# Softmax attention of one query, forward and backward: row broadcast ahead of the K scores, row maxima spread by one transpose, V chunks reordered

## The chip, the cores and the metric

The kernel runs on one core of a Trainium2 chip. The metric is the device time in microseconds, median of several executions. One execution of each kernel was also taken with the hardware profiler; its span is 1.7 to 2.9 us shorter than the time of the same execution. The granted clock is the share of full speed that the profile shows TensorE was granted.

## The reference

```python
B, H, Sq, Skv, Dh = 1, 32, 1, 8192, 128          # bfloat16
def fwd(q, k, v):
    scores = einsum('bhqd,bhkd->bhqk', q, k) * Dh ** -0.5
    return einsum('bhqk,bhkd->bhqd', softmax(scores), v)
def reference(q, k, v, grad_out):
    out, vjp = jax.vjp(fwd, q, k, v)
    return (out, *vjp(grad_out))                 # out, dq, dk, dv
```

A head has one query, 8192 keys and 8192 values. Each head reads K and V (2 MiB each) once and writes dK and dV (2 MiB each) once: 8.39 MB per head, 268.4 MB in all.

## The kernel before

A head's K and V lie on 128 partitions with 64 slots of 128 elements each. VectorE transposes K, TensorE makes the scores, softmax follows, TensorE transposes V in four chunks and makes the products with it, and VectorE writes dV = p x grad_out and dK = ds x q, which are stored. The program works on head h while it finishes dK of head h-1. In the profile lines, XK_sb is the transposed K, s_ps the scores, mx and nbias the row maxima, e the exponentials, qd the broadcast rows of q and grad_out, p_rep and ds_rep are p and ds, and G_dv and G_dk are dV and dK on their way out. The parts that the change touches (cut at the dots):

```python
def k_scores(h):
    x = st[h]
    x["s"] = psS.tile([P, 512], F32, tag="s", name="s_ps")     # one PSUM bank
    ...                                                        # 64 matmuls into x["s"][:, 0:NT]

def rows_bc(h):                                                # q and grad_out on all partitions
    x = st[h]
    nc.tensor.matmul(x["m"][:, 256:512], lhsT=ident[0:H, h:h + 1].to_broadcast([H, P]),
                     rhs=rows[:].rearrange("h a d -> h (a d)"), start=True, stop=True, ...)
    x["qd"] = small.tile([P, 2, D], BF16, tag="qd", name="qd")
    nc.scalar.copy(x["qd"][:].rearrange("p a d -> p (a d)"), x["m"][:, 256:512])

for h in range(H + 1):
    p_ = h - 1
    if h < H:
        x = st[h] = {}
        for u in range(NCH):
            k_blocks(h, u)                       # VectorE transposes of K
        k_scores(h)
    ...                                          # ds, first parts of dK and dq of head h-1
    if 0 < h and h + 2 < H:
        load_k(h + 2)                            # 3 K buffers
    if h < H:
        nc.vector.reduce_max(mx[:], x["sn"], axis=AX.X)
        nc.vector.tensor_scalar(diag[:], ident_f[:], mx[:], scale, op0=ALU.mult, op1=ALU.mult)
        nc.tensor.matmul(x["m"][:, 128:256], lhsT=ones_f[:], rhs=diag[:], ...)
        rows_bc(h)
    if h > 0:
        outer(p_, "dk", 2)
    if h < H:
        nc.vector.tensor_reduce(nbias[:], x["m"][:, 128:256], axis=AX.X, op=ALU.max, negate=True)
        nc.scalar.activation(e[:], x["sn"], ACT.Exp, bias=nbias[:], scale=scale, accum_out=rs[:])
    ...
    v_transposes(h, 0); v_transposes(h, 1)       # each: 8 transposes on TensorE, one ScalarE copy
    contract(Vt[h], x["p"], x["m"][:, 2:3])      # O: 64 matmuls
    v_scores(h, 0)
    v_transposes(h, 2)
    ...                                          # one product with grad_out
    v_scores(h, 1)
    v_transposes(h, 3)
    v_scores(h, 2); v_scores(h, 3)
    for r in range(4): outer(h, "dv", r)         # the store follows the last part
```

Of the kernel before, what the change touches and what calls it, by code (L numbers as in the profile page):

```python
# [9 lines left out]
ALU = mybir.AluOpType  # L10
AX = mybir.AxisListType
BF16 = mybir.dt.bfloat16
F32 = mybir.dt.float32
# [10 lines left out]
def kernel(  # L24
# [11 lines left out]
    nc = tc.nc  # L36
    P = 128
    _, H, S, D = k.shape
# [7 lines left out]
    scale = float(D) ** -0.5  # L46
# [7 lines left out]
    small = ctx.enter_context(tc.tile_pool(name="small", bufs=2))  # L54
    psT = ctx.enter_context(tc.tile_pool(name="psT", bufs=2, space=PSUM))
    psS = ctx.enter_context(tc.tile_pool(name="psS", bufs=1, space=PSUM))
# [19 lines left out]
    def load_v(h):  # L76
        Vt[h] = vpool.tile([P, NT, D], BF16, tag="V", name="Vt")
        nc.sync.dma_start(Vt[h][:], rows_of(v, h, 0, 1))
# [9 lines left out]
    ident = consts.tile([P, P], BF16)  # L88
# [5 lines left out]
    ones_f = consts.tile([P, P], F32)  # L94
# [19 lines left out]
    ident_f = consts.tile([P, P], F32)  # L114
# [10 lines left out]
    def do_columns():  # L125
        for e2 in range(2):
            nc.scalar.copy(
                twice[:, e2], rows[:, 1, :].rearrange("h (j e) -> h e j", e=2)[:, e2:e2 + 1, :].to_broadcast([H, 2, W]))
        tp = psT.tile([P, CH, P], BF16, tag="T", name="tp_do")
        for e2 in range(2):  # L130
            nc.tensor.transpose(tp[:, e2, 0:H], twice[:, e2].rearrange("h t j -> h (t j)"), ident[0:H, 0:H])
        nc.tensor.transpose(tp[:, 2, 0:H], rows[:, 1, :], ident[0:H, 0:H])
        for e2 in range(2):
            for t in range(2):
                nc.scalar.copy(do_blk[t * W:(t + 1) * W, :, e2, t], tp[t * W:(t + 1) * W, e2, 0:H])
        nc.scalar.copy(do_f[:], tp[:, 2, 0:H])
# [4 lines left out]
    def k_blocks(h, u):  # L141


        if u == 0:
            XK[h] = ktpool.tile([P, CH, NB, NCH, QD], F32, tag="XK", name="XK_sb")
        nc.vector.transpose(XK[h][:, :, :, u, :],  # L146
                            slots(Kt[h], u, NCH).rearrange("p g d -> p (g d)").bitcast(F32).rearrange(
                                "p (g w j) -> p g w j", g=CH, w=NB))

    def k_scores(h):  # L150
        x = st[h]
        x["s"] = psS.tile([P, 512], F32, tag="s", name="s_ps")
        out = x["s"][:, 0:NT].rearrange("p (a g) -> p g a", a=NQ)
        cols = XK.pop(h).rearrange("p g w u i -> p (g w u i)").bitcast(BF16).rearrange(
            "p (g w ui e) -> p g w e ui", g=CH, w=NB, e=2)
        for g in range(CH):
            for c in range(2 * NB):
                nc.tensor.matmul(out[:, g, :], lhsT=cols[:, g, c // 2, c % 2], rhs=q_blk[:, h, c, :],  # L158
                                 start=(c == 0), stop=(c == 2 * NB - 1), skip_group_check=True)
# [18 lines left out]
    def v_transposes(h, c):  # L178

        T_ps = psT.tile([P, CH // 2, P], F32, tag="T", name="T_ps")  # L180
        words = Vt[h].rearrange("p n d -> p (n d)").bitcast(F32)
        for i in range(CH // 2):
            m = c * CH // 2 + i
            nc.tensor.transpose(T_ps[:, i, :], words[:, m * P:(m + 1) * P], ident_f[:])  # L184
        X = tpool.tile([P, CH // 2, P], F32, tag="XT", name="XT_sb")
        nc.scalar.copy(X[:], T_ps[:])  # L186
        XV[h, c] = X

    def v_scores(h, c):
        X = XV.pop((h, c)).rearrange("p m s -> p (m s)").bitcast(BF16).rearrange("p (m s e) -> p m e s", s=P, e=2)  # L190
        if c == 0:
            st[h]["dp"] = psD.tile([P, 512], F32, tag="dp", name="dp_ps")
        for i in range(CH // 2):
            n = c * CH + 2 * i
            for e2 in range(2):
                nc.tensor.matmul(st[h]["dp"][:, n:n + 2], lhsT=X[:, i, e2, :], rhs=do_blk[:, h, e2, :],  # L196
                                 start=(e2 == 0), stop=(e2 == 1), skip_group_check=True)

    def contract(Xt, rep, out_col, first=0, last=NT):
        for n in range(first, last):  # L200
            nc.tensor.matmul(out_col, lhsT=Xt[:, n, :], rhs=rep[:, n, 0:1],  # L201
                             start=(n == 0), stop=(n == NT - 1), skip_group_check=True)
# [19 lines left out]

    def rows_bc(h):
        x = st[h]
        nc.tensor.matmul(x["m"][:, 256:512], lhsT=ident[0:H, h:h + 1].to_broadcast([H, P]),  # L225
                         rhs=rows[:].rearrange("h a d -> h (a d)"), start=True, stop=True,
                         skip_group_check=True)
        x["qd"] = small.tile([P, 2, D], BF16, tag="qd", name="qd")
        nc.scalar.copy(x["qd"][:].rearrange("p a d -> p (a d)"), x["m"][:, 256:512])  # L229

    def ds_of(h):
        x = st[h]
# [7 lines left out]
    def dq_of(h, half):  # L240
        out = st[h]["dp"][:, 128:129]
        contract(Kt[h], st[h]["ds"], out, half * NT // 2, (half + 1) * NT // 2)
        if half == 1:
            nc.scalar.copy(dq_all[:, h:h + 1], out)  # L244
# [10 lines left out]
    for h in range(H + 1):  # L255
        p_ = h - 1
        if h < H:
            x = st[h] = {}
            for u in range(NCH):
                k_blocks(h, u)  # L260
            k_scores(h)
        if h == 0:
            do_columns()
        if h > 0:
            ds_of(p_)
            outer(p_, "dk", 0)
            dq_of(p_, 0)
        if h < H:
            s_mask(h)
            s_swap(h)  # L270
        if h > 0:
            dq_of(p_, 1)
            outer(p_, "dk", 1)
        if 0 < h and h + 2 < H:
            load_k(h + 2)
        if h < H:
            mx = small.tile([P, 1], F32, tag="mx")
            nc.vector.reduce_max(mx[:], x["sn"], axis=AX.X)
            diag = small.tile([P, P], F32, tag="diag")
            nc.vector.tensor_scalar(diag[:], ident_f[:], mx[:], scale, op0=ALU.mult, op1=ALU.mult)  # L280
            x["m"] = psM.tile([P, 512], F32, tag="m", name="m_ps")
            nc.tensor.matmul(x["m"][:, 128:256], lhsT=ones_f[:], rhs=diag[:], start=True, stop=True,  # L282
                             skip_group_check=True)
            rows_bc(h)
        if h > 0:
            outer(p_, "dk", 2)
        if h == 0:
            load_k(2)
        if h < H:
            nbias = small.tile([P, 1], F32, tag="nbias")  # L290
            nc.vector.tensor_reduce(nbias[:], x["m"][:, 128:256], axis=AX.X, op=ALU.max, negate=True)  # L291
            e = small.tile([P, NT], F32, tag="e")
            rs = small.tile([P, 1], F32, tag="rs")
            nc.scalar.activation(e[:], x["sn"], ACT.Exp, bias=nbias[:], scale=scale, accum_out=rs[:])  # L294
            nc.tensor.matmul(x["m"][:, 0:1], lhsT=ones_f[:], rhs=rs[:], start=True, stop=True,  # L295
                             skip_group_check=True)
        if h > 0:
            outer(p_, "dk", 3)
        if h == H:
            break  # L300
        rinv = small.tile([P, 1], F32, tag="rinv")
        nc.vector.reciprocal(rinv[:], x["m"][:, 0:1])  # L302
        x["p"] = small.tile([P, NT, R], BF16, tag="prep", name="p_rep")
        nc.scalar.activation(x["p"][:], e[:].unsqueeze(2).to_broadcast([P, NT, R]), ACT.Copy, scale=rinv[:])  # L304
        x["p_s"] = small.tile([P, NT], F32, tag="p_s", name="p_s")
        nc.vector.tensor_scalar(x["p_s"][:], e[:], rinv[:], scale, op0=ALU.mult, op1=ALU.mult)
        v_transposes(h, 0)
        v_transposes(h, 1)
        contract(Vt[h], x["p"], x["m"][:, 2:3])
        nc.scalar.copy(o_all[:, h:h + 1], x["m"][:, 2:3])  # L310
        v_scores(h, 0)
        v_transposes(h, 2)
        nc.tensor.matmul(x["m"][:, 1:2], lhsT=do_f[:, h:h + 1].to_broadcast([P, P]), rhs=o_all[:, h:h + 1],
                         start=True, stop=True, skip_group_check=True)
        v_scores(h, 1)
        v_transposes(h, 3)
        v_scores(h, 2)
        v_scores(h, 3)
        outer(h, "dv", 0)
        outer(h, "dv", 1)  # L320
        outer(h, "dv", 2)
        if 0 < h and h + 2 < H:
            load_v(h + 2)
        outer(h, "dv", 3)
        if h == 0:
            load_v(2)
        if h == H - 1:
            result(o_all, out_0)
# [33 lines left out]
```

## Time and profile before

| | before |
|---|---|
| time, median of 3 runs | 647.68 us (646.88 to 647.79) |
| span of the profiled run | 646.4 us |
| busy: VectorE, TensorE, ScalarE | 79%, 77%, 29% |
| data moved, share of 16 DMA engines | 268.47 MB, 97.9% |

"Share of 16 DMA engines" adds the durations of all packets and divides by 16 spans. From the list of who waited for whom (waiter, what ended the wait, us in total, times, longest us):

```profile
PE s_ps L158 <- DVE pdt L234: 50.4, 25, 3.7
DVE nbias L291 <- ACT qd L229: 20.6, 32, 2.0
```

The first is TensorE idle ahead of the K scores. (The wait is for the K transposes; pdt is the VectorE instruction right after them.) The second is VectorE waiting for qd, the copy of the row broadcast.

### The profile page before, as it was taken

How to read it: one execution, taken by the hardware profiler on the slowest of the kernel's cores; microseconds unless marked ns; L12 is line 12 of the kernel's file. 1: busy time of each engine (PE TensorE's matmuls, PEld its weight loads, DVE VectorE, ACT ScalarE, POOL GpSimd, SP SyncE). 2: the span in 40 equal slices, each digit the busy share in tenths (PEclk: the TensorE clock that was granted, in tenths of full speed). 3: DMA queues.
4: the chain of work that ended last, by engine and by line, in shares of the span. 5: the costliest groups of instructions: out<-in, count | busy, mean ns of one | idle time of the engine just before them, and what ended most of it. 6: DMA issues, size and time to landing. Idle time of an engine off the chain costs nothing.

```text
span 646.4 us, 20967 instructions
## 1 busy us (share of the span) xinstructions
PE 500.6 (77%) x9705; PEld 468.8 (73%) x9705; DVE 512.2 (79%) x653; ACT 184.7 (29%) x332; POOL 0.7 (0%) x6
## 2 busy tenths in 40 slices
PE   2888888788879867788768698767787788877880
PEld 1888787688878756778757687767686787866880
DVE  5888889899877779777798777898777977778851
ACT  2333233233233222232222322223322223222230
POOL 0000000000000000000000000000000000000000
PEclk9765556766655656755566755576755555655555
DMA  8999999999999999999999999999999999999985
GB/s 341 415 426 427 427 420 425 431 424 426 427 428 428 427 431 424 427 430 428 427 428 431 425 427 429 429 429 426 427 429 426 428 429 428 425 429 430 409 358 216
DMA packets 19719, 269.81 MB, mean 417 GB/s; under 512 B 2352, under 2 KB 2352, under 8 KB 2864
## 3 DMA queue, kind: packets, MB, share of 16 engines
q1 hardware_dynamic: 19584, 268.47, 97.9%
q8 instruction: 76, 1.25, 0.7%
q14 instruction: 11, 0.09, 0.0%
q10 hardware_dynamic: 48, 0.01, 0.0%
HBM read 134.23 MB, written 134.23 MB: 415 GB/s over the span
## 4 chain that ended last, share of the span: by engine, by line
DMA 58%; PE 23%; DVE 13%; ACT 2%; issue 1%; SPq 0%; DVEq 0%; ACTq 0%
DMA Kt<-in_k_dram 58%; DVE XK_sb L146 10%; PE T_ps L184 6%; PE s_ps L158 6%; PE dp_ps L201 5%; PE m_ps L201 2%; DVE G_dv L211 1%; PE dp_ps L196 1%; PE s_ps L174 1%; ACT XT_sb L186 1%; PE m_ps L282 1%; DVE G_dk L211 1%; PE m_ps L295 1%; ACT qd L229 0%; PE m_ps L225 0%
## 5 line engine op out<-in xcount | busy, mean ns | idle before, releaser
L184 PE MATMUL T_ps<-ident_f,Vt 128*128 128x128 f32 x1024 | 216.2, 391 | 0.0
L211 DVE TENSOR_TENSOR G_dv<-p_rep,qd 128x2048 bf16<-128x2048 bf16 x128 | 148.2, 1220 | 68.7 <-DMA out_dram<-G_dv 66.5
L184 PEld LDWEIGHTS T_ps<-ident_f,Vt 128*128 128x128 f32 x1024 | 191.8, 213 | 0.0
L186 ACT COPY XT_sb<-T_ps 128x1024 f32<-128x1024 f32 x128 | 129.6, 1013 | 142.1 <-PE T_ps L184 142.1
L211 DVE TENSOR_TENSOR G_dk<-ds_rep,qd 128x2048 bf16<-128x2048 bf16 x128 | 155.7, 1218 | 1.1
L146 DVE STREAM_TRANSPOSE XK_sb<-Kt 128x1024 f32<-128x1024 f32 x128 | 148.2, 1214 | 7.4 <-DMA Kt<-in_k_dram 6.9
L158 PE MATMUL s_ps<-q_blk,XK_sb 128*128 128x4 bf16 x2048 | 59.5, 168 | 58.2 <-DVE pdt L234 50.4
L158 PEld LDWEIGHTS <-XK_sb 128*128 128x128 bf16 x2048 | 56.9, 104 | 60.4 <-DVE pdt L234 52.4
L196 PEld LDWEIGHTS <-XT_sb 128*128 128x128 bf16 x2048 | 71.7, 104 | 28.9 <-ACT XT_sb L186 27.4
L196 PE MATMUL dp_ps<-do_blk,XT_sb 128*128 128x2 bf16 x2048 | 72.7, 165 | 24.7 <-ACT XT_sb L186 24.7
L201 PE MATMUL dp_ps<-ds_rep,Kt 128*128 128x1 bf16 x2048 | 64.4, 165 | 2.9 <-issue 2.5
L201 PEld LDWEIGHTS <-Kt 128*128 128x128 bf16 x2048 | 59.7, 104 | 8.4 <-issue 8.2
L244 ACT COPY dq_all<-dp_ps 128x1 f32<-128x1 f32 x32 | 5.1, 159 | 199.9 <-PE dp_ps L201 199.9
L201 PEld LDWEIGHTS <-Vt 128*128 128x128 bf16 x2048 | 60.2, 101 | 1.5
L201 PE MATMUL m_ps<-p_rep,Vt 128*128 128x1 bf16 x2048 | 58.7, 165 | 0.0
L295 PEld LDWEIGHTS m_ps<-rs,ones_f 128*128 128x128 f32 x64 | 16.0, 311 | 48.6 <-ACT e L294 48.6
L295 PE MATMUL m_ps<-rs,ones_f 128*128 128x1 f32 x64 | 18.7, 362 | 39.2 <-ACT e L294 39.2
L282 PE MATMUL m_ps<-diag,ones_f 128*128 128x128 f32 x64 | 25.4, 501 | 0.7 <-DVE diag L280 0.7
L291 DVE TENSOR_REDUCE nbias<-m_ps 128x1 f32<-128x128 f32 x32 | 9.3, 292 | 20.6 <-ACT qd L229 20.6
L304 ACT ACTIVATE p_rep<-e,rinv 128x256 bf16<-128x256 f32 x32 | 16.3, 508 | 30.0 <-DVE rinv L302 30.0
L236 DVE SCALAR_TENSOR_TENSOR ds_rep<-dp_ps,pdt,p_s 128x256 bf16<-128x256 f32 x32 | 15.5, 484 | 11.3 <-PE dp_ps L196 8.7
L229 ACT CAST qd<-m_ps 128x256 bf16<-128x256 f32 x32 | 11.9, 372 | 30.5 <-PE m_ps L225 30.5
(44 smaller groups left out, 155.0 us busy)
## 6 DMA issues: line engine op xcount, KB each, us to landing
Vt<-in_v_dram SPq DMA_DIRECT2D x32, 2048.0 KB, 28.2
Kt<-in_k_dram SPq DMA_DIRECT2D x31, 2048.0 KB, 30.7
out_dram<-G_dv SPq DMA_DIRECT2D x30, 2048.0 KB, 32.8
out_dram<-G_dk SPq DMA_DIRECT2D x30, 2048.0 KB, 32.9
out_dram<-G_dv SPq DMA_DIRECT2D x4, 1024.0 KB, 14.0
out_dram<-G_dk SPq DMA_DIRECT2D x4, 1024.0 KB, 12.0
Kt<-in_k_dram SPq DMA_DIRECT2D x4, 512.0 KB, 5.5
out_dram<-fin_sb SPq DMA_DIRECT2D x2, 8.0 KB, 11.9
```

What stands on the lines that cost most here:

```text
L146: nc.vector.transpose(XK[h][:, :, :, u, :], slots(Kt[h], u, NCH).rearrange("p g d -> p (g d)").bitcast(F32).rearrange("p (g w j) -> p g w ...
L158: nc.tensor.matmul(out[:, g, :], lhsT=cols[:, g, c // 2, c % 2], rhs=q_blk[:, h, c, :], start=(c == 0), stop=(c == 2 * NB - 1), skip_group ...
L184: nc.tensor.transpose(T_ps[:, i, :], words[:, m * P:(m + 1) * P], ident_f[:])
L186: nc.scalar.copy(X[:], T_ps[:])
L196: nc.tensor.matmul(st[h]["dp"][:, n:n + 2], lhsT=X[:, i, e2, :], rhs=do_blk[:, h, e2, :], start=(e2 == 0), stop=(e2 == 1), skip_group_chec ...
L201: nc.tensor.matmul(out_col, lhsT=Xt[:, n, :], rhs=rep[:, n, 0:1], start=(n == 0), stop=(n == NT - 1), skip_group_check=True)
L211: nc.vector.tensor_tensor(slots(G, r, 4).rearrange("p n (a b) -> p n a b", b=R), slots(rep, r, 4).unsqueeze(2).to_broadcast([P, Q, D // R, ...
L229: nc.scalar.copy(x["qd"][:].rearrange("p a d -> p (a d)"), x["m"][:, 256:512])
L236: nc.vector.scalar_tensor_tensor(out=x["ds"][:], in0=x["dp"][:, 0:NT].unsqueeze(2).to_broadcast([P, NT, R]), scalar=pdt[:], in1=x["p_s"][: ...
L282: nc.tensor.matmul(x["m"][:, 128:256], lhsT=ones_f[:], rhs=diag[:], start=True, stop=True, skip_group_check=True)
L295: nc.tensor.matmul(x["m"][:, 0:1], lhsT=ones_f[:], rhs=rs[:], start=True, stop=True, skip_group_check=True)
L304: nc.scalar.activation(x["p"][:], e[:].unsqueeze(2).to_broadcast([P, NT, R]), ACT.Copy, scale=rinv[:])
```

## The change

The intent is to shorten the chain from the row maxima to the exponential, and to close gaps in the V part.

```diff
     def k_scores(h):
         x = st[h]
-        x["s"] = psS.tile([P, 512], F32, tag="s", name="s_ps")
@@ rows_bc
-        nc.tensor.matmul(x["m"][:, 256:512], lhsT=ident[0:H, h:h + 1].to_broadcast([H, P]),
+        x["s"] = psS.tile([P, 512], F32, tag="s", name="s_ps")
+        nc.tensor.matmul(x["s"][:, 256:512], lhsT=ident[0:H, h:h + 1].to_broadcast([H, P]),
...
-        nc.scalar.copy(x["qd"][:].rearrange("p a d -> p (a d)"), x["m"][:, 256:512])
+        nc.scalar.copy(x["qd"][:].rearrange("p a d -> p (a d)"), x["s"][:, 256:512])
@@ the loop over heads
             x = st[h] = {}
+            rows_bc(h)
             for u in range(NCH):
...
-            diag = small.tile([P, P], F32, tag="diag")
-            nc.vector.tensor_scalar(diag[:], ident_f[:], mx[:], scale, op0=ALU.mult, op1=ALU.mult)
+            top = small.tile([P, 1], F32, tag="top")
+            nc.vector.tensor_scalar_mul(top[:], mx[:], scale)
...
-            nc.tensor.matmul(x["m"][:, 128:256], lhsT=ones_f[:], rhs=diag[:], start=True, stop=True,
-                             skip_group_check=True)
-            rows_bc(h)
+            nc.tensor.transpose(x["m"][:, 128:256], top[:].to_broadcast([P, P]), ident_f[:])
...
         v_transposes(h, 1)
+        v_transposes(h, 2)
         contract(Vt[h], x["p"], x["m"][:, 2:3])
         nc.scalar.copy(o_all[:, h:h + 1], x["m"][:, 2:3])
         v_scores(h, 0)
-        v_transposes(h, 2)
+        v_scores(h, 1)
+        v_transposes(h, 3)
         nc.tensor.matmul(x["m"][:, 1:2], ...)
-        v_scores(h, 1)
-        v_transposes(h, 3)
         v_scores(h, 2)
```

## The prediction

> **What bounds the kernel now.** I read the page first: its DMA rows and its table of DMA queues.
>
> ```profile
> DMA  8999999999999999999999999999999999999985
> q1 hardware_dynamic: 19584, 268.47, 97.9%
> HBM read 134.23 MB, written 134.23 MB: 415 GB/s over the span
> ```
>
> The reader is to see that the 16 DMA engines are busy in every fortieth of the run but the first and the last two, and that the packets of the one data queue take 97.9% of 16 engines' time: 0.979 x 646.4 = 632.8 us. Only 646.4 - 632.8 = 13.6 us of the span is not transfer. No rearrangement of compute can win more than that unless it moves fewer bytes, and the change moves the same ones: 32 heads x (K, V in; dK, dV out) x 2 MiB = 268.4 MB.
>
> Next I read the table of stretches, 20 us each, to see where those 13.6 us lie. Columns: stretch, length, busy time of each engine, granted TensorE clock, DMA share, GB/s.
>
> ```profile
> 0.00:20.00 20.00, 7.37 (x97) 6.28 (x98) 10.68 (x25) 4.87 (x13) 0.70 (x6) 1.00 0.91 358
> ...
> 300.00:320.00 20.00, 16.65 (x305) 15.64 (x304) 15.95 (x20) 5.66 (x10) 0.00 (x0) 0.50 1.00 427
> ...
> 600.00:620.00 20.00, 16.79 (x318) 15.78 (x316) 16.09 (x21) 5.86 (x11) 0.00 (x0) 0.50 0.92 392
> 620.00:640.00 20.00, 9.46 (x202) 8.95 (x199) 9.52 (x10) 3.99 (x9) 0.00 (x0) 0.50 0.83 345
> ```
>
> From 20 to 600 us the share is 1.00 or 1.01 in every stretch, at 415 to 430 GB/s. What is missing lies at the two ends: 0.09 x 20 = 1.8 us at the start, 0.08 x 20 + 0.17 x 20 = 5.0 us in the last two stretches, and most of the 6.4 us after 640. A head is 8.39 MB, at 427 GB/s 19.6 us; its K loads are issued every 19.8 us.
>
> Then the chain of waits, which says how compute and transfers lock together (start us, length, what):
>
> ```profile
> 373.93 0.96 PE dp_ps L201 x32
> 374.89 0.02 issue
> 374.91 30.90 DMA Kt<-in_k_dram
> 405.80 0.02 issue
> 405.82 4.62 DVE XK_sb L146 x4
> 410.45 0.06 DVE pdt L234
> 410.50 0.00 issue
> 410.51 1.87 PE s_ps L158 x64
> 412.38 0.85 PE dp_ps L201 x32
> 413.23 0.37 PE s_ps L174 x8
> 413.60 0.96 PE dp_ps L201 x32
> 414.56 0.02 issue
> 414.57 30.75 DMA Kt<-in_k_dram
> ```
>
> The reader is to see a loop of two heads, 39.7 us: a K load of 30.9 us, then 8.8 us of compute that frees a K buffer and issues the next load. A 2 MiB transfer at 427 GB/s is 4.9 us, so 30.9 us from issue to landing is a queue of about six transfers. Whatever compute saves only makes the next load wait longer in that queue. Of the instructions that the change touches, none is in this loop: its line numbers (282, 225, 229, and the order of 184, 196, 201, 313 in the V part) stand in the chain only before 141 us and after 613 us.
>
> **What the Trainium skill says.** "DMA: Bandwidth & Descriptors", section Specifications, gives 435 GB/s as the ceiling of the fabric and about 358 as the memory limit per core. The trace agrees with the first, 427 GB/s being 98% of it; it exceeds the second. The same page, "Why a DMA increments its semaphore by 16 and not by 1", says that the engines of one transfer finish independently and that it is done only when all are. The tail agrees: the store of dV of head 29, issued at 585.75, is what G_dv waited for until 619.71 (34 us), though at 612 to 616 the mean share had fallen to 0.67 and 0.64. Some engines had run dry, others lagged. "PSUM — Partial Sum Buffer", section "PSUM bank collisions raise a hardware error", says that two engines' accesses to one bank must be kept apart, reads too. The trace agrees: nbias (VectorE, reading the maxima) waits in all 32 heads for qd (ScalarE, reading other columns of the same tile), 20.6 us in total.
>
> **The change part by part.** I use the last head, where compute is on the path, before:
>
> ```profile
> 612.97 0.28 DVE L280 TENSOR_SCALAR diag<-ident_f,mx 128x128 f32<-128x128 f32 x1
> 613.31 0.80 PE L282 MATMUL m_ps<-diag,ones_f 128*128 128x128 f32 x2
> 614.04 0.39 PE L225 MATMUL m_ps<-rows,ident 32*128 32x256 bf16 x1
> 614.87 0.29 DVE L291 TENSOR_REDUCE nbias<-m_ps 128x1 f32<-128x128 f32 x1 [0.48 <-ACT qd L229]
> ```
>
> Row maxima: the 128x128 diag (0.28 us) becomes a 128x1 multiply, which I size by the 128x1 copy pdt, 0.12 us. The ones matmul in two passes (0.80 us) becomes one f32 transpose, sized by the V transposes' mean of 0.39 us. Row broadcast: its matmul (0.39 us) and its copy qd (0.37 us) leave the space between maxima and nbias; they go ahead of the K scores, into a TensorE wait there, 50.4 us over 25 heads, about 2 us each. New cost: the K scores share a bank with qd now and wait for it. In the first heads, where that TensorE wait is absent, this puts back about 0.34 + 0.38 + two hand-overs of 0.04 = 0.8 us.
>
> How early does nbias come? Not by the whole 0.34 + 0.38 + 0.4 us. VectorE runs a piece of G_dk (1.22 us) between diag and nbias, from 613.17 to 614.39; it starts 0.1 to 0.15 us earlier with the smaller multiply, so nbias can start at about 614.28 in place of 614.87. That is **0.6 us** for exp, p and all behind it.
>
> V part: the TensorE sum is the same. Before, the last transposes end at 626.14, the copy runs 626.22 to 627.24, and the last scores start at 627.28; TensorE idles 0.76 us there. After, only the 0.22 us product of line 313 moves from ahead of those transposes into that idle time (0.22 + 0.43 of scores fits in 1.1 us of copy). The third transposes now stand ahead of the contraction, but they need only the first copy, which ended 0.66 us before they could start. Gain **0.2 us**.
>
> Sum for the last head: ds and the last two stores 0.6 + 0.2 = 0.8 us earlier. For the first head, where VectorE has no G_dk to do: exp at about 15.0 in place of 16.39, 1.3 us, so the first store comes at 19.3 in place of 20.67. The upfront loads, 5 x 2.1 MB at 427 GB/s, keep the engines busy to about 27 us; at 26 to 32 us the rate is 377, 397 and 410 GB/s, a loss of (50 + 30 + 17) x 2 us = 0.19 MB, 0.45 us. The earlier store may recover about half of that, 0.2 us. Heads 1 to 30: nothing.
>
> **The rivals.** (1) The DMA tail is set by the lagging engines, which still have dV to write when dK comes. For it: share 0.56 and 0.64 at 628 to 632, when stores were outstanding, and a drain that runs to 642 and beyond though the last data store is issued at about 633. Then the 0.8 us of the last head are worth nothing, and the time is 647.5. (2) The tail follows the last issue one for one: 647.68 - 0.8 - 0.2 = 646.7. Against it: the same lag. (3) The kernel is bound by TensorE (77% busy) and each head gains 0.6 to 0.8 us: 32 x 0.7 = 22 us, 625 us. Against it: the share of 1.00 and the queue of six; 625 us is below the transfer time of 632.8. (4) The new wait of the K scores or the changed order starves the queue: a head would have to take over 19.8 us. The first heads, not yet held back by transfers, took 17 to 20 us of compute and the change adds no net work. I see no way to 2% slower.
>
> **Range and chances.** Between rivals 1 and 2 I choose the middle, 647.1 us. The three runs before spread over 0.9 us, another chip or session may shift by 0.3% (about 2 us, my guess for it), so 645.2 to 648.8. Two per cent is 13 us, as much as all time that is not transfer: faster 0.01, slower 0.01, same 0.98.
>
> **What would show each step right or wrong.** The data queue's time stays at 632 to 634 us and the share at 1.00 from 20 to 600 us. K loads still come every 19.8 us, and time from issue to landing is the same or slightly longer. In the last head, nbias starts 0.5 to 0.7 us earlier relative to the landing of the last K and waits for nothing but its own engine, and the last G_dk about 0.8 us earlier. The transpose shows 32 matmuls of 0.3 to 0.45 us in place of 64. In the first heads, the K scores wait for qd. The prediction is wrong if the rate in the middle leaves 427 GB/s, if the drain after the last store gets longer or shorter by over 2 us, or if the share falls below 1.00 in mid-run.

## The result and the profile after

| | before | after |
|---|---|---|
| time, median of 4 runs each | 647.73 us (646.88 to 647.96) | 646.49 us (646.33 to 646.59) |
| span of the profiled run | 646.4 us | 644.5 us |
| TensorE busy | 500.6 us | 481.0 us |
| VectorE busy | 512.2 us | 505.5 us |

The ratio of the times is 0.9983, with a 95% interval from 0.9966 to 1.0. Ratios in this document are the mean time of one kernel's runs over that of the other's in the same rounds, so not quite the ratio of the medians quoted. The time is inside the predicted range: 1.2 us less, of which the interval leaves anything from nothing to 2.2 us. TensorE's busy time fell by 20 us and the kernel's by 1.2.

The page of the changed kernel, its DMA rows:

```profile
DMA  8999999999999999999999999999999999999985
q1 hardware_dynamic: 19584, 268.47, 98.2%
HBM read 134.23 MB, written 134.23 MB: 417 GB/s over the span
```

0.982 x 644.5 = 632.9 us of transfer, against 632.8 before: the same work, with 11.6 us of other time in place of 13.6. The table of stretches (length, busy time of TensorE, its weight loads, VectorE, ScalarE and GpSimd, granted clock, DMA share, GB/s):

```profile
300.00:320.00 20.00, 15.25 (x304) 14.38 (x303) 15.73 (x21) 5.68 (x11) 0.00 (x0) 0.57 1.01 428
...
600.00:620.00 20.00, 14.65 (x288) 13.56 (x285) 14.93 (x21) 5.12 (x11) 0.00 (x0) 0.58 0.96 408
620.00:640.00 20.00, 6.48 (x191) 6.02 (x188) 8.47 (x9) 2.89 (x8) 0.00 (x0) 0.59 0.79 330
```

In this stretch TensorE is busy for 15.25 us in 20 in place of 16.65, with a granted clock of 0.57 in place of 0.50 (from 160 to 580 us the means are 15.1 and 15.8 us, at 0.59 and 0.57), and DMA moves 428 GB/s in place of 427. The chain of waits shows why that is worth nothing there:

```profile
194.90 30.84 DMA Kt<-in_k_dram
...
225.76 4.62 DVE XK_sb L146 x4
...
230.44 1.87 PE s_ps L157 x64
...
234.50 30.84 DMA Kt<-in_k_dram
```

The loop is still 39.6 us for two heads, and a K load still takes 30.8 us from issue to landing, six transfers deep in the queue. (From 425 us on the chain passes twice through a store, of 35.3 and 34.4 us, in place of a K load.)

In the last head (start us, length, engine, line, operation, and in brackets the idle time before it):

```profile
609.02 1.23 DVE L210 TENSOR_TENSOR G_dk<-ds_rep,qd 128x2048 bf16<-128x2048 bf16 x1 [1.00 <-DMA out_dram<-G_dk]
...
611.88 0.15 DVE L281 TENSOR_SCALAR top<-mx 128x1 f32<-128x1 f32 x1
...
612.09 0.48 PE L283 MATMUL m_ps<-ident_f,top 128*128 128x128 f32 x1
...
613.08 0.28 DVE L290 TENSOR_REDUCE nbias<-m_ps 128x1 f32<-128x128 f32 x1
```

nbias no longer waits for qd. But VectorE stood still for 1.00 us earlier in this head, waiting for a dK buffer whose store was still in the queue.

**Where the 1.2 us came from.** The K transposes of the last head started at 604.65 us before and at 602.76 after: the whole difference of the two spans, 1.9 us, is already there. From that point to the end of the span it is 41.76 us before and 41.72 us after, although the last dK was computed 28.40 us after that point before and only 27.20 us after it now. The earlier stores were taken up by a longer drain.

The trace also records, for every transfer, 16 landing marks, one for each DMA engine; a transfer is complete at the 16th. I sorted them by time, for the load of the last K (us):

| | first engine | 8th | 15th | 16th | 16th minus first |
|---|---|---|---|---|---|
| before | 588.3 | 601.2 | 602.1 | 604.6 | 16.3 |
| after | 588.5 | 600.5 | 602.4 | 602.7 | 14.2 |

So the 16 engines do not run in step. Some seven of them are far ahead of the rest by the end, and the slowest one, which decides when a transfer is done, lags by 14 to 16 us. The mean share of 1.00 hides it, because until about 612 us none of them runs dry. The engines that are ahead are no faster after the change (588.3, 588.5); the slowest one is 1.9 us faster.

From this come two theories. **ENDS**: the gain came from the first and last head, where compute is not hidden. **LAG**: the DMA engine that lags most has work from 2 us to the end without a pause, so the kernel ends when that engine has done its sum of packets; compute at the ends is worth nothing, and the 1.2 us are a change in this engine's load.

### The profile page after: what moved, and what is told of

Its sections match the earlier page's. It is cut to its first block, busy times and chain, and to the rows that moved or that the text cites. A ratio compares the mean times of both kernels' runs of the same rounds, so it can differ in the third digit from the quotient of the medians.

```text
span 644.5 us, 20935 instructions
## 1 busy us (share of the span) xinstructions
PE 481.0 (75%) x9673; PEld 452.0 (70%) x9673; DVE 505.5 (78%) x653; ACT 183.5 (28%) x332; POOL 0.7 (0%) x6
## 3 DMA queue, kind: packets, MB, share of 16 engines
q8 instruction: 75, 1.23, 0.7%
## 4 chain that ended last, share of the span: by engine, by line
DMA 59%; PE 21%; DVE 14%; ACT 2%; issue 1%; SPq 0%; DVEq 0%; ACTq 0%
DMA Kt<-in_k_dram 48%; DVE XK_sb L146 8%; PE T_ps L183 8%; DMA out_dram<-G_dv 5%; DMA out_dram<-G_dk 5%; PE s_ps L157 5%; DVE G_dk L210 4%; PE dp_ps L200 3%; PE m_ps L200 2%; PE dp_ps L195 2%; ACT XT_sb L185 1%; PE m_ps L294 1%; DVE G_dv L210 1%; PE s_ps L173 1%; DVE sm L163 1%
## 5 line engine op out<-in xcount | busy, mean ns | idle before, releaser
L183 PE MATMUL T_ps<-ident_f,Vt 128*128 128x128 f32 x1024 | 203.4, 382 | 0.2 <-PE m_ps L294 0.2
L195 PE MATMUL dp_ps<-do_blk,XT_sb 128*128 128x2 bf16 x2048 | 66.7, 164 | 18.1 <-ACT XT_sb L185 18.1
L195 PEld LDWEIGHTS <-XT_sb 128*128 128x128 bf16 x2048 | 64.9, 102 | 20.7 <-ACT XT_sb L185 20.7
L200 PEld LDWEIGHTS <-Vt 128*128 128x128 bf16 x2048 | 57.7, 97 | 0.9
L200 PE MATMUL m_ps<-p_rep,Vt 128*128 128x1 bf16 x2048 | 56.9, 164 | 0.0
L303 ACT ACTIVATE p_rep<-e,rinv 128x256 bf16<-128x256 f32 x32 | 16.3, 508 | 30.1 <-DVE rinv L301 30.1
L163 DVE TENSOR_TENSOR sm<-s_ps,in_quad 128x256 f32<-128x256 f32 x32 | 13.6, 424 | 11.1 <-PE s_ps L157 7.9
L229 ACT CAST qd<-s_ps 128x256 bf16<-128x256 f32 x32 | 11.9, 372 | 32.2 <-PE s_ps L225 32.2
L293 ACT ACTIVATE e<-s_ps,nbias 128x64 f32<-128x64 f32 x32 | 10.0, 313 | 31.8 <-DVE nbias L290 31.8
## 6 DMA issues: line engine op xcount, KB each, us to landing
Kt<-in_k_dram SPq DMA_DIRECT2D x31, 2048.0 KB, 30.8
```

What stands on the lines that cost most here:

```text
L163: nc.vector.tensor_tensor(x["sm"][:], x["s"][:, 0:NT].rearrange("p (a g) -> p a g", a=NQ).unsqueeze(2) .to_broadcast([P, NQ, NCH, CH]), in ...
L183: nc.tensor.transpose(T_ps[:, i, :], words[:, m * P:(m + 1) * P], ident_f[:])
L195: nc.tensor.matmul(st[h]["dp"][:, n:n + 2], lhsT=X[:, i, e2, :], rhs=do_blk[:, h, e2, :], start=(e2 == 0), stop=(e2 == 1), skip_group_chec ...
L200: nc.tensor.matmul(out_col, lhsT=Xt[:, n, :], rhs=rep[:, n, 0:1], start=(n == 0), stop=(n == NT - 1), skip_group_check=True)
L303: nc.scalar.activation(x["p"][:], e[:].unsqueeze(2).to_broadcast([P, NT, R]), ACT.Copy, scale=rinv[:])
```

## The experiments

Twelve kernels ran, each timed in rounds beside the kernel before, 4 to 6 runs each (median of before: 648.07 us with the first four, 648.25 with the next four, 648.04 to 648.09 with the last four). All were correct except one. The changed kernel was not timed again: differences from it are across sessions, in which the kernel before rose by 0.3 to 0.5 us.

### The three parts, each alone

`row_only` moves rows_bc ahead of the K scores and into their tile, and leaves the rest as before:

```diff
+        x["s"] = psS.tile([P, 512], F32, tag="s", name="s_ps")       # in rows_bc, no longer in k_scores
-        nc.tensor.matmul(x["m"][:, 256:512], ...
+        nc.tensor.matmul(x["s"][:, 256:512], ...
```

> The kernel before with the row broadcast alone moved ahead of the K scores and into their tile. Two theories. ENDS: the 1.2 us that the change gained came from the first and last head, where compute is not hidden. LAG: the end is set by the DMA engine that lags most; it is never idle between 2 us and the end, so compute at the ends is worth nothing and the 1.2 us are that engine's own luck or load. ENDS expects 0.5 to 1.0 us less than before (nbias 0.6 us earlier in the last head, 0.75 us in the first). LAG expects a difference that does not follow the last head: the time from the landing of the last K to the end of the span stays at 41.8 us, as in both profiles, though ds of the last head comes about 0.6 us earlier after that landing.

`max_only` replaces the diagonal and the product with ones by the multiply and the transpose:

```diff
...                                                            # diag becomes top, as in the change
-            nc.tensor.matmul(x["m"][:, 128:256], lhsT=ones_f[:], rhs=diag[:], ...)
+            nc.tensor.transpose(x["m"][:, 128:256], top[:].to_broadcast([P, P]), ident_f[:])
```

> The kernel before with the transpose of the row maxima alone (32 matmuls fewer). ENDS expects 0.3 to 0.5 us less than before. LAG expects no relation to the part: 41.8 us from the landing of the last K to the end, and any gain already there at that landing.

`v_only` has the new order of the V part alone:

```diff
+        v_transposes(h, 2)
         contract(Vt[h], x["p"], x["m"][:, 2:3])
...
         v_scores(h, 0)
-        v_transposes(h, 2)
+        v_scores(h, 1)
+        v_transposes(h, 3)
...                                                            # their old places further down go
```

> The kernel before with the new order of the V part alone. ENDS expects 0.2 us less than before, within noise of nothing. LAG expects 41.8 us from the landing of the last K to the end, and any gain or loss already there at that landing.

| | time us | ratio to before (95%) | ds after the last K's transposes began | end after they began |
|---|---|---|---|---|
| row_only | 647.70 | 0.9992 (0.9979 to 1.0004) | 20.36 | 41.73 |
| max_only | 646.83 | 0.9981 (0.9969 to 0.9994) | 22.84 | 41.64 |
| v_only | 647.22 | 0.9987 (0.9975 to 1.0) | 21.84 | 41.72 |
| before | | | 23.25 | 41.76 |
| after | | | 22.05 | 41.72 |

The kernel whose last head came earliest (row_only: ds 2.9 us earlier than before) gained least, and max_only, in which ds came 0.4 us earlier, gained most, though their intervals overlap, so that order is not shown. (Of the 2.9 us only 0.5 are the part's own, up to nbias. The rest is the clock: from nbias to ds it was granted 0.81, against 0.50 before.) What is shown is that the end stays at 41.6 to 41.8 us whatever ds does. That is what LAG said and not what ENDS said.

### Earlier work at the end

`tail_early` is the changed kernel with a third dV buffer and the last head's stores in quarters.

```diff
+    dvpool = ctx.enter_context(tc.tile_pool(name="gdv", bufs=3))
-            x[which] = gpool.tile([P, NT, D], BF16, ...)
+            x[which] = (gpool if which == "dk" else dvpool).tile([P, NT, D], BF16, ...)
+        if h == H - 1:
+            parts = 4
```

> The changed kernel with a third buffer for dV (the last head's dV need not wait for a store that is 34 us in the queue) and the last head's stores in quarters. The last head's dV should be issued some 3 us earlier and the first part of its dK 1.2 us earlier. ENDS expects 1 to 2.5 us less than the changed kernel (644.0 to 645.5). LAG expects the engines that were ahead to run out later and the last one to end at the same time: within 0.5 us of the changed kernel (646.0 to 647.0).

It took 646.69 us (ratio 0.9976 to before, 0.9962 to 0.999), 0.2 us more than the changed kernel had, which is within the drift of the sessions. The last stores, from the DMA issues in order of time:

```profile
616.93 4.21 SPq L223 DMA_DIRECT2D out_dram<-G_dv  x4
...
626.97 8.33 SPq L223 DMA_DIRECT2D out_dram<-G_dk  x4
```

dV starts to go out at 616.9 in place of 621.05, dK at 627.0 in place of 627.7. The engines that were ahead finished the last dK at 637.5 in place of 633.9, as they had more to do in quarters that came late (the four issues took 8.33 us). The slowest one finished at 643.6 in place of 643.2. Neither the first issue nor the last moved the end.

### More compute in the loop

`loop_delay` is the changed kernel with one more VectorE product in heads 1 to 30:

```diff
+            if 0 < h < H - 1:
+                idle = small.tile([P, 2048], BF16, tag="idle", name="idle")
+                nc.vector.tensor_tensor(idle[:]..., slots(Kt[h], 0, 4), slots(Kt[h], 1, 4), op=ALU.mult)
```

> The changed kernel with a VectorE product of 128x2048 elements (1.2 us) in each of heads 1 to 30, between the K transposes and ds, so in the loop from the landing of a K load to the issue of the next. If the loop were the bound, 15 turns of two heads would take 15 to 30 x 1.2 us = 18 to 36 us more. If the queue of transfers absorbs compute, as predicted, the time from issue to landing of the K loads falls from 30.8 to about 29.6 us and the kernel takes the same time within 0.7 us.

It took 647.00 us (ratio 0.998, 0.9966 to 0.9993), and VectorE worked 32 us more. Its chain of waits:

```profile
210.97 1.10 DVE idle L264
...
215.80 30.18 DMA Kt<-in_k_dram
...
255.45 30.20 DMA Kt<-in_k_dram
```

The loop is still 39.65 us. Its compute grew by 0.7 us, from 8.8 to 9.5 (I had put 1.2, the length of the product; a part of it fell into waits that the loop had anyway), and the load's time fell by 0.66 us, from 30.84 to 30.18. The queue of transfers takes up compute and gives it back, one for one.

### What makes an engine lag

The DMA queues of the page show, besides the data queue, two instruction queues, through which the unrolled program itself is read from memory. In the changed kernel (queue, kind: packets, MB, share of 16 engines):

```profile
q8 instruction: 75, 1.23, 0.7%
q14 instruction: 11, 0.09, 0.0%
```

The Trainium skill, "Runtime: NRT & Kernel Launch", section Instruction fetch mechanics, says that an engine's instructions are refilled in blocks of 16 KiB, 256 instructions, by a DMA queue of its own. The trace agrees: 19,346 TensorE instructions x 64 bytes are 1.24 MB, and q8 moved 1.23 MB in 75 packets. One such packet took 0.88 to 1.07 us, in which its DMA engine moves no data: from 60 to 588 us, 15.1 data packets were in flight on average while one instruction packet was, and 16.1 while none was, in the kernel before, the changed kernel, few_instr and pool_fetch alike. (A data packet of 16 KB takes 0.611 us.) Two kernels change that load.

`few_instr`: contractions over every fourth slot, so its result is wrong.

```diff
-        for n in range(first, last):
+        for n in range(first, last, 4):
```

> The changed kernel with both contractions over every fourth slot only; its result is wrong on purpose. TensorE has 96 matmuls and 96 weight loads fewer per head (some 2.5 us of work), and 6,144 instructions fewer in all, 0.39 MB at 64 bytes, which is 24 of the 75 packets of 16 KB in the instruction queue. A theory of TensorE as the bound expects about 10% less time (580 to 600 us). LAG with lag from the instruction packets, which share some 8 of the 16 DMA engines (those that land late), expects the slowest engine to end 2 to 4 us earlier (642.5 to 644.5). LAG from another cause expects the time of the changed kernel, 646.5, within 0.7.

`pool_fetch`: 128 tiny memsets in each of heads 1 to 30 on GpSimd, which does nothing else in a head.

```diff
+            if 0 < h < H - 1:
+                for _ in range(128):
+                    nc.gpsimd.memset(spare[:], 0.0)
```

> The changed kernel with 128 memsets of one column per head on GpSimd, which is idle otherwise: 3,840 instructions more, 0.25 MB, about 15 more packets of 16 KB in an instruction queue, on an engine that nothing waits for. LAG with lag from the instruction packets expects 1 to 3 us more than the changed kernel (647.5 to 649.5) and the growth in the slowest DMA engine alone. ENDS and LAG from another cause expect 646.5 within 0.7.

few_instr took 642.90 us (ratio 0.9917, 0.9903 to 0.993), pool_fetch 653.11 us (1.0074, 1.0061 to 1.0086). The instruction queues of few_instr:

```profile
q8 instruction: 51, 0.84, 0.5%
q14 instruction: 11, 0.09, 0.0%
```

and of pool_fetch:

```profile
q8 instruction: 75, 1.23, 0.8%
q14 instruction: 41, 0.34, 0.1%
```

| landing marks of the last K, us | first | 8th | 15th | 16th | 16th minus first |
|---|---|---|---|---|---|
| after | 588.5 | 600.5 | 602.4 | 602.7 | 14.2 |
| few_instr | 589.6 | 596.9 | 599.6 | 600.8 | 11.2 |
| pool_fetch | 588.4 | 601.0 | 608.0 | 609.4 | 21.1 |

With 24 packets fewer, the nine last marks come 1.9 to 3.6 us earlier (the seven first 1.0 to 2.0 later) and the kernel 3.6 us earlier. TensorE lost 94 us of work for it (481 to 387 us), so TensorE is not the bound; the theory that it is expected 580 to 600 us. In few_instr the lag of the slowest engine grows in jumps of mostly 1.1 to 1.6 us with flat stretches between, one for a fetched block, it seems.

With 30 packets more, on an engine that nothing waits for, the two last marks come 5.6 and 6.7 us later, the 5th to 7th, which had lagged by 0.4 to 4.9 us, 1.2 to 7.5 us, the other eleven move by under 1 us, and the kernel takes 6.6 us more. GpSimd was busy for 378 us with its memsets, but a general slowing by them would show in the first marks, and these stay (588.4 and 588.5). (I expected 1 to 3 us from 15 packets; there were 30 packets, of 8 KB where the page has 16 KiB for every engine, and they fell on few engines.)

The marks are sorted anew in each kernel, so a mark is not always the same engine. Added up over all 16 marks, few_instr is 17 us earlier for 22 packets fewer by then and pool_fetch 28 us later for 30 more, 0.8 and 0.9 us a packet. (The 8 KB packets themselves took only 0.31 to 0.45 us, so a part of their cost lies elsewhere.) The kernel before is only 3.5 us later than the changed one in this sum, 1.9 of it in the slowest engine. So fetched instructions are a load that some DMA engines bear and others don't, and the slowest of them sets the time.

Over all profiled kernels whose stores were not cut by partitions, the span is the lag of the last K's 16th mark plus a constant: 630.1 before, 630.3 after, 629.7 row_only, 629.6 max_only, 629.9 v_only, 629.8 tail_early, 629.8 loop_delay, 629.8 few_instr, 630.0 pool_fetch, and of those that follow, 629.9 nudge, 629.7 nudge_60, 631.2 after_nudge. This joins two things that hardly vary, the first engine's mark (587.9 to 589.6) and the time from the 16th to the end, so it is a summary and no further proof.

### Can an idle edit earn as much?

`nudge` is the kernel before with 28 more tiny transposes at the start, while TensorE waits for K anyway: 56 instructions that shift all later ones within their blocks. `nudge_60` has 60 of them, and `after_nudge` is the changed kernel with 28.

```diff
+    spare = psT.tile([P, CH, P], BF16, tag="T", name="spare")
+    for c in range(28):
+        nc.tensor.transpose(spare[:, c % CH, 0:H], four[:, c % (2 * NB)].rearrange("h a j -> h (a j)"), ident[0:H, 0:H])
```

> The kernel before with 28 more small transposes (56 TensorE instructions) at the start, while TensorE waits for K anyway; nothing that any head does is changed. PARTS (some part of the change earns the 1.2 us) expects the time of before, within 0.3 us. LUCK (the end is one DMA engine's sum of packets, and any edit that shifts when and on which engine instruction blocks are fetched moves it by one packet, 1 to 1.5 us) expects a gain or loss of up to 1.5 us with the landing of the last K moved by as much, and 41.7 us from there to the end as in all runs with whole last stores.

> The kernel before with 60 idle transposes at the start in place of 28. PARTS expects the time of before within 0.3 us. LUCK expects a value from 646 to 649 that need not be that of the first nudge, with 41.7 us from the landing of the last K to the end.

> The changed kernel with the same 28 idle transposes at the start that took 1.1 us off the kernel before. PARTS (the change itself earns its 1.2 us) expects 646.5 within 0.3 us, and about 1.1 us less if the nudge is a gain of its own that adds up (645.4). LUCK expects any value from 645.5 to 648, with 41.7 us from the landing of the last K to the end.

| | time us | ratio to before (95%) | lag at the last K | end after the last K's transposes began |
|---|---|---|---|---|
| nudge | 646.99 | 0.998 (0.9968 to 0.9993) | 15.3 | 41.78 |
| nudge_60 | 647.78 | 0.9992 (0.9978 to 1.0005) | 16.2 | 41.77 |
| after_nudge | 646.24 | 0.9973 (0.9961 to 0.9986) | 12.8 | 41.76 |

An edit that changes nothing in any head took 1.1 us off the kernel before, nearly all that the change took, and another such edit 0.3 us. The changed kernel, tail_early, loop_delay and after_nudge lie at 646.2 to 647.0, the kernel before and its two nudges at 647.0 to 648.3. So the change may own a part of its 1.2 us; these runs cannot say how much, as it is of the size of an idle edit. If it owns one, it gets it through the lag: 41.7 us at the end are the same in all of these kernels.

### Two attempts at relieving the engines that lag

`last_dk_8` cuts the second half of the last dK into 16 transfers of 8 partitions, `balance` cuts two of the last stores into 49, 49 and 30 partitions. By the Trainium skill, "DMA: Bandwidth & Descriptors", section Why a DMA increments its semaphore by 16 and not by 1, a transfer uses the largest number of engines up to 16 that divides its number of partitions, so 8 or 7 here, and I hoped that these were the engines that are ahead. (The traces fit the count: with the 8-partition transfers alone left, from 640 us, at most 8 engines were busy at the moments that I sampled.)

```diff
+            if h == H - 1 and which == "dk" and c == parts - 1:                  # last_dk_8
+                for g in range(0, P, 8):
+                    nc.sync.dma_start(to[g:g + 8], of[g:g + 8])
```

```diff
+            if (h == H - 2 and which == "dv") or (h == H - 1 and which == "dk" and c == 0):   # balance
+                for lo, hi in ((0, 49), (49, 98), (98, P)):
+                    nc.sync.dma_start(to[lo:hi], of[lo:hi])
```

> The changed kernel with the second half of the last dK, 1 MB, as 16 transfers of 8 partitions each, which should run on 8 of the 16 DMA engines. LAG expects the end to move by one engine's share of that transfer, 8 packets of 8 KB at 0.31 us = 2.4 us: 2.4 us earlier (644.1) if these 8 engines are the ones that are ahead, later by as much (648.9) if they are the ones that lag, later by 2 more where the 16 issues take longer than the lag. ENDS, where the end follows the last issue, expects 3 to 5 us more, for 15 more issues of 0.34 us.

> The changed kernel with two of the last stores (dV of head 30 and the first half of the last dK) cut by partitions into 49, 49 and 30, so that the first two run on 7 DMA engines each, those that seem to be ahead, and the third on 15. An engine that lags is freed of 3.65 + 1.8 = 5.5 us of packets at 0.61 us per 16 KB, an engine that is ahead gets 7.3 us more and has about 6 us of idle time and 6 to 9 us of lead. LAG expects the end 3.5 to 5.5 us earlier than in the changed kernel (641.0 to 643.0). ENDS expects no gain, as no instruction of compute comes earlier: 646.5 or more.

last_dk_8 took 650.57 us (1.0035, 1.0023 to 1.0048). Its 16 issues took 15.4 us, till 645 us, so they and not the lag set its end. Its 4.1 us more than the changed kernel lie where ENDS expected them, and where LAG did for issues that outlast the lag: it decides nothing between the theories. balance took 661.15 us (1.0196, 1.0182 to 1.021), 14.7 us more than the changed kernel, where LAG as I applied it had expected 3.5 to 5.5 us less. Its table of stretches:

```profile
612.00:628.00 16.00, 13.26 (x237) 12.41 (x234) 10.87 (x15) 5.95 (x13) 0.00 (x0) 0.61 0.95 331
628.00:644.00 16.00, 0.00 (x0) 0.00 (x0) 1.98 (x2) 0.25 (x1) 0.00 (x0) 0.50 0.69 243
```

The engines are 0.95 busy in the first stretch but move 331 GB/s. The trace has data packets of 16 KB there that took 1.23 us, twice the usual 0.611. From 645 us on only some four engines had data left, until 657. So the assumptions failed: it seems that of the 7 engines that got the work some were ones that lag, and transfers cut this way ran at half speed in part. The three issues of the first half of the last dK also took 11.24 us, so that its second half was issued at 639.93 us, against 629.99 in the changed kernel; how much of the 14.7 us each of these cost was not separated. This does not contradict LAG, as the kernel again ended with its most loaded engines, but it does not confirm it either. No correct version here beats both kernels by more than the idle edits scatter.

## Why the prediction was right or wrong

**What bounds the kernel: right.** The data queue took 632.9 us, the share stayed at 1.00 to 1.02 from 20 to 600 us, the loop stayed at 39.6 us, and compute that was saved in heads 1 to 30 did not reach the end. few_instr and loop_delay show it in both directions.

**The tail: rival 1 was right, and the middle that I chose was too generous.** The prediction gave half of the last head's 0.8 us to the time. The measured value is nothing: it was 41.6 to 41.8 us from the last K to the end in eleven kernels with their last stores whole or in quarters, with ds anywhere from 20.4 to 23.3 us after it. Only few_instr needed less, 40.1 us, probably because it has fewer blocks to fetch in this part too. By the time alone rival 2 (646.7) would look right; that 646.49 lies near it is luck, as the 1.2 us were there before the tail began.

**nbias in the last head: wrong.** I had it 0.59 us earlier. It came 10.32 us after the K transposes began, against 10.22 before, because the first piece of G_dk waited 1.00 us for its buffer. In an ordinary head the step holds: K transposes at 324.80 and nbias at 334.38, 9.58 us, against 326.67 and 336.89, 10.22 us, before: 0.64 us earlier, as worked out. In loop_delay, pool_fetch and after_nudge, which contain the change, the last head's nbias had no such wait and came after 9.58 to 9.59 us too. In ordinary heads row_only gave 0.49 us and max_only 0.42: together less than their sum, as predicted, for VectorE's piece of G_dk stands in between.

**The V part: hardly a gain.** I had 0.2 us. From nbias to ds it was 13.04 us before and 11.73 after, 1.3 us less, but nearly all of that is clock: the granted clock was 0.98 and 0.87 at 620 to 624 us and 0.50 before, which I had not looked for. nudge and nudge_60 have the old order, and in their last heads the clock from nbias to ds was 0.65 as in the changed kernel: they took 11.71 and 11.73 us. v_only, with the new order at 0.65, took 11.63. So the order is worth 0.1 us or nothing. With the new order the clock from nbias to the last scores was about 0.65 in 29 to 31 of 32 heads, while with the old one it was 0.50 in 8 to 13 heads and up to 0.86 in others; why was not tested.

**Single durations: about right.** The transpose took 0.48 us (predicted 0.39, with 0.3 to 0.45 as the sign of being right, so just outside), the multiply 0.15 us (0.12). The K scores do wait for qd in the first heads, seven times 0.46 us, and TensorE starts them 0.85 us after the row broadcast began (predicted 0.8).

**The start: wrong.** The first store was issued at 18.88 in place of 20.67 us. I had given it 0.2 us of the end. Adding up what the DMA engines had moved, the changed kernel was level with the one before at 40 us (386 and 387 GB/s until then).

**What was missing.** The gain that was measured, 1.2 us, is none of the terms of the sum. The sum counted the DMA engines as one; it saw that they lag in the tail, but took the lag for a given. It is a quantity that an edit shifts by 1 to 2 us, and the whole difference lies in it. The prediction's range held because it allowed for 2 us of this kind, which it put down to chips and sessions. The Trainium skill, "Perfetto Trace Analysis", section What "DMA-bound" means, lists specific DMA engines first among the things that bind; these runs agree, and a mean share of 1.00 is not enough to see it.

**What stays open:** which engine fetches which block. The trace does not name the DMA engine of a packet, so the 1.9 us between before and after were not traced to single fetched blocks; the number of packets alone does not order the kernels (76 in before and in nudge, 75 in the changed kernel).

## What to carry to other kernels

Where transfers fill the DMA engines from start to end, only the load of the slowest engine is worth work: look at the spread of the landing marks of one transfer, not only at the mean share. In such a kernel a long unrolled program is itself a load on some of the engines, so instructions saved can be worth more than busy time saved. And a gain of 0.2% needs an idle edit beside it before it is put down to its cause.

## What the Trainium skill lacked or had wrong

- "Runtime: NRT & Kernel Launch", section Instruction fetch mechanics, calls the cost of crossing a 16 KiB boundary mostly hidden. That does not hold for the DMA engines that carry the blocks: 24 blocks fewer were worth 3.6 us here, 30 packets more for an otherwise idle engine (of 8 KB each, not 16) cost 6.6 us, and the engines spread by 14 to 16 us.
